# A decode attention block with a gated FFN: key and value tiles of four heads instead of two, three buffers instead of five, FFN and output weights last

## The chip, the cores and the metric

The kernel runs on one core of a Trainium2 chip (trn2). The metric is the device time of one execution in microseconds (us). A core has five engines with a queue each: TensorE (PE; its weight loads are listed as PEld), VectorE (DVE), ScalarE (ACT), GpSimd (POOL) and SyncE (SP), which here issues every DMA. Sixteen DMA engines, shared by all queues, move data between HBM and SBUF, the core's memory of 128 partitions; PSUM takes the results of TensorE.

## The reference

```python
q = (x @ wq)                       # x: [4, 1, 512], wq: [512, 32 heads * 128]
scores = einsum(q, k_cache) * 128 ** -0.5      # k_cache, v_cache: [4, 32, 4096, 128]
o = einsum(softmax(scores), v_cache)
a = o.reshape(4, 1, 4096) @ wo                 # wo: [4096, 512]
b = (gelu(x @ w_gate) * (x @ w_up)) @ w_down   # inner width 1792
g = sigmoid((x * gate_w).sum(-1, keepdims=True))
out = g * a + (1 - g) * b
```

All is float32. There are 4 batch entries with one query each; each has 32 heads with keys and values of their own, 4096 rows of 128 numbers. The two caches are 537 MB of the 565 MB that are read, and each number of them is used once.

## The kernel before, in words

**Tiles.** A key tile holds two heads of one batch entry (`HT = 2`): each head's 4096 rows lie over 64 partitions, 64 rows (`R`) of 128 numbers in each, so a partition gets 32 KB in one piece and a tile is 4 MB. Value tiles have the same layout. There are 64 tiles of each kind (index `i`: head pair `g = i // 4`, batch entry `b = i % 4`). All big loads share five places of 32 KB per partition (`NB = 5`, pool `kv`): the two halves of wq, keys, values, w_gate, w_up and w_down.

**Order.** The kernel is written in a manual schedule: on each engine the instructions stand in the order of the Python text, and an instruction waits for the data it reads and for the place that it writes. SP issues the big loads in the order of the list `loads`: wq in two halves (L62), then keys one tile ahead of values (L60), w_gate and w_up (L64) after the tiles 19 and 20, w_down (L69) last. Beside them go x (L95), gate_w in 13 small pieces (L104), and wo in 16 loads of 512 KB in rows of 2 KB, one for each head pair (L91).

**Scores.** The queries are computed at the start (L154 products with wq, L162 transposes, L164 copies into `QT`). `q_spread` (L177, L180) lays the queries of two heads for all four batch entries over the partitions, in `QB`. `products` (L192) multiplies 14 rows of a key tile by the query on DVE into a buffer `pr`, and `sums` (L198) adds each row up on DVE; 8 of the 64 rows (buffer `pa`) are added up by ACT instead (L201). In the last two tiles ACT adds up 24.

**Softmax.** `max_a` takes each partition's maximum (L217) and turns it into one row by a PE transpose (L219). `soft_max` takes the maximum of each head (L224), spreads it by PE (L227), copies it (L229) and has ACT compute the exponentials and their sums (L232) into one of three weight buffers `PM`. `soft_sum` (L239) adds up the sums over partitions.

**Values.** `pv` (L257) multiplies weights by values: 16 products of 128x512, four at a time on four column groups of PE, each recorded twice, so 32 records a tile. `o_out` copies the result (L264) and gathers the heads (L268); `weigh` (L277, L280) divides by the sums, and `project_a` (L250) multiplies by the rows of wo that belong to the two heads, adding up over the head pairs in `a_acc`.

**FFN.** `ffn_up` (L299), `ffn_gelu` (L307 to L320) run between the tiles 20 and 22, in a place of the pool. `ffn_down` (L250, `b_acc`) runs in parts around the last value tile. The last instructions are the gate's two products (L368, L372) and the store (L373).

**Loop.** In iteration `i` the program order is: first products of tile `i`, softmax of tile `i - 1`, products and sums of tile `i`, the next load, `pv(i - 1)`, the next load, `o_out(i - 1)`, `max_a(i)`, then the small loads and every fourth time `q_spread`.

Of the kernel before, what the change touches and what calls it, by code (L numbers as in the profile page):

```python
# [17 lines left out]
def tile_gated_mix(ctx: ExitStack, tc: tile.TileContext, x, kc, vc, wq, wo, w_gate, w_up, w_down, gate_w, out):  # L18
    nc = tc.nc
# [5 lines left out]
    C4 = DM // 4  # L25
    HT = 2
    PH = P // HT
    R = S // PH
    NT = B * H // HT
    NB = 5  # L30
    TW = R * D
    RJ = 4

    MANY = (((56, 64),), ((0, 14), (14, 28), (28, 42), (42, 56)), ("A0", "D0", "D1", "D2", "D3"))
    LAST = (((40, 48), (48, 56), (56, 64)), ((0, 14), (14, 28), (28, 40)), ("A0", "A1", "D0", "A2", "D1", "D2"))
    NL = 2
    FFN_AT = 20
    FG = 512
    GW_CUTS = (15, 14, 13, 12, 11, 10, 9, 8, 7, 6, 5, 4, 14)
# [3 lines left out]
    consts = ctx.enter_context(tc.tile_pool(name="consts", bufs=1))  # L43
    kv = ctx.enter_context(tc.tile_pool(name="kv", bufs=NB))
    work = ctx.enter_context(tc.tile_pool(name="work", bufs=2))
    ps2 = ctx.enter_context(tc.tile_pool(name="ps2", bufs=2, space=PSUM))
    ps1 = ctx.enter_context(tc.tile_pool(name="ps1", bufs=1, space=PSUM))
    ctx.enter_context(tc.manual_schedule())

# [3 lines left out]
    def load(kind, i):  # L53
        t = T[kind, i] = kv.tile([P, TW], F32, name="kv")
        if kind in "kv":
            h, b = HT * (i // B), i % B
            src = (kc if kind == "k" else vc)[b, h:h + HT].rearrange("h (p r) d -> (h p) (r d)", p=PH)
            n = 2 if (kind, i) == ("v", NT - 1) else 1
            for s in range(n):
                nc.sync.dma_start(t[:, s * TW // n:(s + 1) * TW // n], src[:, s * TW // n:(s + 1) * TW // n])  # L60
        elif kind == "q":
            nc.sync.dma_start(t, wq.rearrange("(p c) n -> p (c n)", c=KC)[:, i * TW:(i + 1) * TW])  # L62
        elif kind == "f":
            nc.sync.dma_start(t[:, :KC * F], (w_gate, w_up)[i].rearrange("(p c) n -> p (c n)", c=KC))  # L64
        else:
            for f0 in range(0, F, FG):
                f1 = min(f0 + FG, F)
                n = (f1 - f0) // P
                nc.sync.dma_start(t[:, f0 // P * DM:(f0 // P + n) * DM],  # L69
                                  w_down[f0:f1].rearrange("(p i) n -> p (i n)", i=n))  # L70

    loads = [("q", 0), ("q", 1), ("k", 0)]
    for i in range(NT):
        if i + 1 < NT:
            loads.append(("k", i + 1))
        loads.append(("v", i))
        if i in (FFN_AT - 1, FFN_AT):
            loads.append(("f", i - FFN_AT + 1))
    loads.append(("d", 0))
    loads = iter(loads)  # L80

    def load_next():
        n = next(loads, None)
        if n:
            load(*n)

    WO = {}

    def load_wo(g):
        WO[g] = work.tile([P, HT, DM], F32, name="wo_sb")  # L90
        nc.sync.dma_start(WO[g], wo[g * HT * D:(g + 1) * HT * D, :].rearrange("(h p) n -> p h n", p=P))  # L91

    load_next()
    x_sb = consts.tile([B, DM], F32)
    nc.sync.dma_start(x_sb, x.rearrange("b s d -> (b s) d"))  # L95
    load_next()
    for _ in range(NB - 2):
        load_next()
    gw = consts.tile([P, KC], F32)
    load_wo(0)  # L100

    def load_gw(j):
        s = slice(sum(GW_CUTS[:j]), sum(GW_CUTS[:j + 1]))
        nc.sync.dma_start(gw[s], gate_w.rearrange("(p c) -> p c", c=KC)[s])  # L104

    ident = consts.tile([P, P], F32)
    make_identity(nc, ident)
    ones = consts.tile([P, P], F32)  # L110
    nc.vector.memset(ones, 1.0)

    sel = consts.tile([P, RJ, HT], F32)
    nc.vector.tensor_reduce(sel.rearrange("p j h -> p (j h)"),
                            ident.rearrange("p (c m) -> p m c", c=4)[:, :RJ * HT, :], axis=AX.X, op=OP.add)

    PM = [consts.tile([P, R, HT], F32, name=f"pm{j}") for j in range(3)]
    RS = [consts.tile([P, B, HT], F32, name=f"rs{j}") for j in range(2)]
    for t in PM + RS:
        nc.vector.memset(t, 0.0)  # L120


    xT_ps = ps2.tile([P, KC, B], F32, name="sm")
    for c in range(KC):
        nc.tensor.transpose(xT_ps[:, c, :], x_sb[:, c::KC], ident[:B, :B])

    xT = consts.tile([P, KC, 4, B, 8], F32)
    for c in range(KC):
        nc.vector.tensor_copy(xT[:, c], xT_ps[:, c, None, :, None].to_broadcast([P, 4, B, 8]))
    xT = xT.rearrange("p c j b k -> p c (j b k)")  # L130
    g_cols = consts.tile([P, 2], F32)

    def gate():
        z = ps2.tile([P, 1], F32, name="sm")
        for c in range(KC):
            nc.tensor.matmul(z, xT[:, c, :], gw[:, c:c + 1], start=c == 0, stop=c == KC - 1)
        ez = work.tile([P, 1], F32, name="m1")
        nc.scalar.activation(ez, z, AF.Exp, scale=-1.0)
        gd = work.tile([P, 1], F32, name="nb")
        nc.vector.tensor_scalar(gd, ez, 1.0, None, op0=OP.add)  # L140
        nc.vector.reciprocal(g_cols[:, 0:1], gd)
        nc.vector.tensor_scalar(g_cols[:, 1:2], g_cols[:, 0:1], -1.0, 1.0, op0=OP.mult, op1=OP.add)


    PO = [ps1.tile([P, RJ, D], F32, name=f"po{j}") for j in range(2)]
    HG = H // 4
    HB = HG // 2
    q_sb = work.tile([P, HG, D], F32, name="wo_sb")
    for c in range(KC):
        w = T["q", c // 2].rearrange("p (c n) -> p c n", c=2)[:, c % 2, :]  # L150
        for s in range(2):
            for j in range(4):
                n0 = (j * HG + s * HB) * D
                nc.tensor.matmul(PO[s][32 * j:32 * j + 32].rearrange("p j d -> p (j d)"), xT[:, c, :32],  # L154
                                 w[:, n0:n0 + HB * D], start=c == 0, stop=c == KC - 1)
    for s in range(2):
        nc.scalar.activation(q_sb[:, s * HB:(s + 1) * HB, :], PO[s], AF.Copy)
    QT = consts.tile([P, 4, HG, B], F32)
    for s in range(2):
        ps = ps1.tile([P, HB, P], F32, name="q")  # L160
        for a in range(HB):
            nc.tensor.transpose(ps[:, a, :], q_sb[:, s * HB + a, :], ident)  # L162
        for a in range(HB):
            nc.vector.tensor_copy(QT[:, :, s * HB + a, :],  # L164
                                  ps[:, a, :].rearrange("p (j b k) -> p j b k", j=4, b=B)[:, :, :, 0])
    QT = QT.rearrange("p j a b -> p (j a) b")
    for _ in range(2):
        load_next()


    QB = {}

    def q_spread(g):
        ps = ps1.tile([P, B, D], F32, name="q")
        for b in range(B):
            for h in range(HT):
                nc.tensor.matmul(ps[h * PH:(h + 1) * PH, b, :], QT[:, HT * g + h, b:b + 1].to_broadcast([P, PH]),  # L177
                                 ident, start=True, stop=True)
        QB[g] = work.tile([P, B, D], F32, name="qb")
        nc.scalar.activation(QB[g], ps, AF.Copy)  # L180


    SC = {}
    dump = consts.tile([P, D], F32)

    def products(i, o):
        a, d, _ = LAST if i >= NT - NL else MANY
        r0, r1 = (a if o[0] == "A" else d)[int(o[1])]
        g, b = divmod(i, B)
        n = r1 - r0  # L190
        t = work.tile([P, n, D], F32, name="pa") if o[0] == "A" else work.tile([P, n, D], F32, name="pr", bufs=1)
        nc.vector.tensor_tensor(t, T["k", i].rearrange("p (r d) -> p r d", d=D)[:, r0:r1],  # L192
                                QB[g][:, b:b + 1, :].to_broadcast([P, n, D]), op=OP.mult)
        return t, r0, r1

    def sums(i, o, t, r0, r1):
        if o[0] == "D":
            nc.vector.tensor_reduce(SC[i][:, r0:r1], t, axis=AX.X, op=OP.add)  # L198
        else:
            for r in range(r0, r1):  # L200
                nc.scalar.activation(dump, t[:, r - r0, :], AF.Copy, accum_out=SC[i][:, r:r + 1])  # L201

    def scores_a(i):
        SC[i] = work.tile([P, R], F32, name="sc")
        return products(i, "A0")

    def scores(i, first):
        sums(i, "A0", *first)
        for o in (LAST if i >= NT - NL else MANY)[2][1:]:
            sums(i, o, *products(i, o))  # L210


    MT = {}

    def max_a(i):
        m1 = work.tile([P, 1], F32, name="m1")
        nc.vector.tensor_reduce(m1, SC[i], axis=AX.X, op=OP.max)  # L217
        MT[i] = ps2.tile([1, P], F32, name="sm")
# [177 lines left out]
```

## Time and profile before

| | |
|---|---|
| time, median of 3 runs | 1328.2 us (1328.17 to 1328.27) |
| span of the profiled execution, first to last instruction | 1328.7 us |
| instructions | 10291 |
| read from HBM | 564.67 MB, 425 GB/s over the span |
| DVE busy | 1142.8 us (86%) |
| PE busy | 544.3 us (41%), granted clock 0.648 of full speed in the mean |

The profile is of one execution of its own; its span is 0.5 us over the median of the runs, so a time worked out inside the profile is about 0.5 us more than what the runs would show. In a row of a timeline stand the start, the duration, the engine, the line, the operation, the tile written and the tile read, the shape and the count; in brackets how long the engine had been idle and what ended that. A row of the groups has the total busy time and the mean duration in ns behind the bar. A row of a DMA queue has the packets, the MB, and the time that the packets took as a share of sixteen engines' time. A packet is one contiguous run of bytes that one DMA engine moves.

### The profile page before, as it was taken

The page shows a single profiled execution, that of the slowest core. Times are in us where ns is not written, and L with a number is a line of the kernel's source. Part 1 is how long each engine was busy: PE and PEld are TensorE (multiplying, and loading weights), DVE is VectorE, ACT ScalarE, POOL GpSimd, SP SyncE. Part 2 cuts the span into 40 slices and gives each one's busy share as a digit, 9 for nine tenths or more (in the row PEclk, how much of TensorE's full clock was granted, in tenths as well). Part 3 has the DMA queues.
Part 4 walks back from the last instruction along what each step waited for, and adds up shares of the span by engine and source line. Part 5 has one row for each costly group of instructions (what it writes and reads, how often), then busy time and mean ns, then how long its engine had stood idle before and what let it go on. Part 6 is the DMA issues. An engine that isn't in the chain of part 4 may idle for free.

```text
span 1328.7 us, 10291 instructions
## 1 busy us (share of the span) xinstructions
PE 544.3 (41%) x3690; PEld 191.0 (14%) x3690; DVE 1142.8 (86%) x783; ACT 338.6 (25%) x1499; POOL 0.7 (0%) x6
## 2 busy tenths in 40 slices
PE   4243443443442553343344243343343344353345
PEld 1011111111110121111111111111111111111112
DVE  0999898898898679889889889889889889889874
ACT  0222222222222122312312212212312312212233
POOL 0000000000000000000000000000000000000000
PEclk9665766666666666766766665675665666665666
DMA  9999999999999999999999999999999999999996
GB/s 411 426 426 433 432 427 427 438 427 428 428 436 427 428 430 434 428 432 427 434 426 432 428 432 433 426 431 429 433 426 430 436 426 427 439 427 427 426 436 275
DMA packets 24414, 565.33 MB, mean 425 GB/s; under 512 B 2712, under 2 KB 2728, under 8 KB 6956
## 3 DMA queue, kind: packets, MB, share of 16 engines
q1 hardware_dynamic: 24364, 564.69, 99.2%
q8 instruction: 29, 0.48, 0.1%
q14 instruction: 21, 0.17, 0.0%
HBM read 564.67 MB, written 0.01 MB: 425 GB/s over the span
## 4 chain that ended last, share of the span: by engine, by line
DMA 71%; DVE 22%; PE 5%; issue 1%; another core or an unknown queue 0%; ACT 0%; SPq 0%; DVEq 0%; ACTq 0%
DMA kv<-in_A_k_cache 50%; DMA kv<-in_A_v_cache 21%; DVE pr L192 11%; DVE sc L198 9%; PE po L257 5%; DVE pa L192 2%; DVE m L224 0%; PE b_acc L250 0%; SPq L60 0%; PE oT L268 0%; ACT pm L232 0%; DVE ot L280 0%; ACT o L264 0%; SPq L62 0%
## 5 line engine op out<-in xcount | busy, mean ns | idle before, releaser
L257 PE MATMUL po<-kv,pm 128*8 128x512 f32 x2048 | 369.0, 887 | 489.3 <-DMA kv<-in_A_v_cache 482.2
L198 DVE TENSOR_REDUCE sc<-pr 128x14 f32<-128x1792 f32 x254 | 512.5, 2018 | 8.7
L192 DVE TENSOR_TENSOR pr<-kv,qb 128x1792 f32<-128x1792 f32 x254 | 512.3, 2017 | 6.4
L264 ACT ACTIVATE o<-po 128x512 f32<-128x512 f32 x64 | 38.2, 597 | 573.2 <-PE po L257 573.2
L192 DVE TENSOR_TENSOR pa<-kv,qb 128x1024 f32<-128x1024 f32 x68 | 83.2, 1224 | 108.6 <-DMA kv<-in_A_k_cache 108.5
L257 PEld LDWEIGHTS po<-kv,pm 128*8 128x8 f32 x2048 | 67.3, 117 | 738.6 <-issue 711.1
L201 ACT ACTIVATE dump<-pa 128x128 f32<-128x128 f32 x544 | 168.3, 309 | 18.1 <-DVE pa L192 1.5
L201 ACT ACTIVATION_READ_ACCUMULATOR dump<-pa 128x1 f32 x544 | 101.3, 186 | 0.0
L268 PE MATMUL oT<-sel,o 128*128 128x2 f32 x512 | 67.4, 254 | 45.5 <-ACT o L264 45.5
L227 PE MATMUL sm<-m,ones 1*64 1x1 f32 x256 | 23.3, 245 | 152.6 <-DVE m L224 152.6
L229 ACT ACTIVATE nb<-sm 128x1 f32<-128x1 f32 x64 | 10.9, 171 | 291.8 <-PE sm L227 291.7
L268 PEld LDWEIGHTS oT<-sel,o 128*128 128x128 f32 x512 | 61.9, 191 | 107.9 <-ACT o L264 107.9
L219 PE MATMUL sm<-ident,m 128*1 128x128 f32 x64 | 18.9, 295 | 72.4 <-DVE m L217 72.2
L232 ACT ACTIVATE pm<-sc,nb 64x64 f32<-64x64 f32 x128 | 44.9, 351 | 2.9
L227 PEld LDWEIGHTS sm<-m,ones 1*64 1x64 f32 x256 | 17.9, 192 | 169.2 <-DVE m L224 166.9
L232 ACT ACTIVATION_READ_ACCUMULATOR pm<-sc,nb 64x1 f32 x128 | 23.7, 185 | 0.0
L180 ACT ACTIVATE qb<-q 128x512 f32<-128x512 f32 x16 | 9.6, 597 | 50.3 <-PE q L177 50.3
L217 DVE TENSOR_REDUCE m<-sc 128x1 f32<-128x64 f32 x64 | 14.1, 220 | 6.6
L224 DVE TENSOR_REDUCE m<-sm 1x2 f32<-1x128 f32 x64 | 17.3, 270 | 2.6 <-PE sm L219 2.6
L177 PE MATMUL q<-ident,QT 128*64 128x128 f32 x256 | 18.7, 291 | 0.6 <-DVE QT L164 0.6
L250 PE MATMUL a_acc<-wo_sb,ot 128*32 128x128 f32 x256 | 16.9, 412 | 0.0
L219 PEld LDWEIGHTS sm<-ident,m 128*1 128x1 f32 x64 | 5.1, 80 | 75.6 <-issue 36.9
(49 smaller groups left out, 99.8 us busy)
## 6 DMA issues: line engine op xcount, KB each, us to landing
kv<-in_A_k_cache SPq DMA_DIRECT2D x64, 4096.0 KB, 42.5
kv<-in_A_v_cache SPq DMA_DIRECT2D x63, 4096.0 KB, 33.8
kv<-in_A_wq SPq DMA_DIRECT2D x2, 4096.0 KB
wo_sb<-in_A_wo SPq DMA_DIRECT2D x16, 512.0 KB, 43.1
kv<-in_A_v_cache SPq DMA_DIRECT2D x2, 2048.0 KB
kv<-in_B_w_gate SPq DMA_DIRECT2D x1, 3584.0 KB
kv<-in_B_w_up SPq DMA_DIRECT2D x1, 3584.0 KB
kv<-in_B_w_down SPq DMA_DIRECT2D x3, 1024.0 KB, 28.6
```

Of the source, the lines that this page charges most:

```text
L177: nc.tensor.matmul(ps[h * PH:(h + 1) * PH, b, :], QT[:, HT * g + h, b:b + 1].to_broadcast([P, PH]), ident, start=True, stop=True)
L192: nc.vector.tensor_tensor(t, T["k", i].rearrange("p (r d) -> p r d", d=D)[:, r0:r1], QB[g][:, b:b + 1, :].to_broadcast([P, n, D]), op=OP.mult)
L198: nc.vector.tensor_reduce(SC[i][:, r0:r1], t, axis=AX.X, op=OP.add)
L201: nc.scalar.activation(dump, t[:, r - r0, :], AF.Copy, accum_out=SC[i][:, r:r + 1])
L219: nc.tensor.transpose(MT[i], m1, ident)
L224: nc.vector.tensor_reduce(m2, MT[i].rearrange("o (h p) -> o h p", h=HT), axis=AX.X, op=OP.max)
L227: nc.tensor.matmul(nbp[h * PH:(h + 1) * PH, :], ones[:1, :PH], m2[:, h:h + 1], start=True, stop=True)
L232: nc.scalar.activation(PM[i % 3][s, :, h], SC[i][s, :], AF.Exp, bias=nb[s, :], scale=scale, accum_out=RS[g % 2][s, b, h:h + 1])
L250: nc.tensor.matmul(acc[32 * c:32 * c + 32, :], t, w[:, c * C4:(c + 1) * C4], start=start, stop=stop)
L257: nc.tensor.matmul(PO[i % 2][32 * c:32 * c + M].rearrange("p j d -> p (j d)"), p[:, j * M:(j + 1) * M], T["v", i][:, j * N:(j + 1) * N], s ...
L264: nc.scalar.activation(o, PO[i % 2], AF.Copy)
L268: nc.tensor.matmul(OT[g][:, b, :], o[:, j, :], sel[:, j, :], start=j == 0, stop=j == RJ - 1)
```

## The change

The body is rewritten around other tiles.

- **Tiles of four heads.** `HT = 4`: a head lies over 32 partitions, 128 rows in each, so that each partition gets 64 KB in one piece, a tile is 8 MB, and there are 32 of each kind. The pool has three places of 64 KB, which begin at an address fixed by a filler. wq is one tile. A tile's keys are loaded, then its values; the third load behind a tile goes into that tile's place, and waits until the tile has been read for the last time.
- **Products in place.** DVE multiplies a whole key tile by the query in one instruction, writing over the keys, and adds up all 128 rows in a second one. ACT adds up rows only in the last tile (32 of 128), where DVE works in four parts.
- **Softmax.** The maximum of a partition is laid out by a 32x32 transpose on DVE and the maximum of a head taken there, negated; the queries are scaled beforehand. The exponentials are four ACT instructions, one for each head, and there is one weight buffer. The PE transpose and spread and the ACT copy are gone.
- **Values.** 32 products a tile as before in shape. The result is copied and one product (`wide`) adds the column groups up into one PSUM tile for the four batch entries; after four tiles `quotients` takes the heads apart and divides. The projection by wo moves behind the loop.
- **Weights last.** Behind the last value tile come w_gate and w_up as one tile, w_down with the first 18 of 32 rows of wo a partition, and the other 14 rows in five pieces (4, 4, 3, 2, 1 rows). The whole FFN and the whole projection are computed behind the last quotient. gate_w is one load of four rows, and the gate is computed at the start, ahead of the queries.

```diff
-    HT = 2
+    HT = 4
-    NB = 5
+    PIECES = (4, 4, 3, 2, 1)
+    CH = 32
+    BASE = 24576
...
+    filler = front.tile([P, (BASE - 16512 - used) // 4], F32)
+    kv = ctx.enter_context(tc.tile_pool(name="kv", bufs=3))
...
+    def load_kv(kind, i):
+        nc.sync.dma_start(place((kind, i)), heads(kc if kind == "k" else vc, i))
...
+    for i in range(NT):
+        LOADS.append(lambda i=i: load_kv("k", i))
+        LOADS.append(lambda i=i: load_kv("v", i))
+    LOADS += [load_ffn_up, load_down, load_last]
...
+    def multiply(i, r0, r1):
+        k = keys(i)[:, r0:r1]
+        nc.vector.tensor_tensor(k, k, QB[:, i % B, None, :].to_broadcast([P, r1 - r0, D]), op=OP.mult)
+    def add_up(i, r0, r1):
+        nc.vector.tensor_reduce(SC[:, r0:r1], keys(i)[:, r0:r1], axis=AX.X, op=OP.add)
...
+    def weights(i):
...
+        nc.vector.tensor_reduce(m1, SC, axis=AX.X, op=OP.max)
...
+        nc.vector.transpose(mt, m1.to_broadcast([P, 32]))
...
+        nc.vector.tensor_reduce(nm, mt, axis=AX.X, op=OP.max, negate=True)
+        for h in range(HT):
+            s = slice(h * PH, (h + 1) * PH)
+            nc.scalar.activation(PM[s, :, h], SC[s, :], AF.Exp, bias=nm[s, :], scale=1.0,
+                                 accum_out=RS[s, b, h:h + 1])
...
+    for i in range(NT):
+        g, b = divmod(i, B)
+        last = i == NT - 1
+        multiply(i, 0, CH if last else R)
+        if i > 0:
+            if b == 0:
+                totals(g - 1)
+            values(i - 1)
+            load_next()
+        if b == 0 and i > 0:
+            quotients(g - 1)
+        if b == B - 1 and not last:
+            spread(g + 1)
+        if last:
+            add_up_beside(i, 0, CH)
+            for r in range(CH, R, CH):
+                multiply(i, r, r + CH)
+                add_up(i, r, r + CH)
+        else:
+            add_up(i, 0, R)
+        weights(i)
+        load_next()
+    load_next()
+    totals(NG - 1)
+    values(NT - 1)
+    load_next()
+    quotients(NG - 1)
...
+    for s, u in enumerate((u0, u1)):
+        up = PO[s][:, :FG]
+        for c in range(KC):
+            for j in range(4):
+                n0 = (s * KC + c) * F + j * FG
+                nc.tensor.matmul(up[32 * j:32 * j + 32], xT[:, c, :], f[:, n0:n0 + FG],
+                                 start=c == 0, stop=c == KC - 1)
+        nc.scalar.activation(u, up, AF.Copy)
...
+    early = [(hT[:, i, :], T["d"][:, i * DM:(i + 1) * DM]) for i in range(DR)]
+    early += [(OW[:, :, i], T["d"][:, (DR + i) * DM:(DR + i + 1) * DM]) for i in range(W1)]
+    for n, (l, r) in enumerate(early):
+        c = n % 4
+        nc.tensor.matmul(a[32 * c:32 * c + B], l, r, start=n < 4, stop=n >= len(early) - 4)
+    a_sb = back.tile([P, DM], F32, name="gs")
+    nc.scalar.activation(a_sb, a, AF.Copy)
...
+    for i in range(W1, WR):
+        for c in range(4):
+            r0 = (i - W1) * DM + c * P
+            nc.tensor.matmul(acc[32 * c:32 * c + 32], OX[:, i - W1].rearrange("p b k -> p (b k)"),
+                             T["w"][:, r0:r0 + P], start=False, stop=i == WR - 1)
```

Names used below: k0 to k31 and v0 to v31 are the new tiles; `values`, `totals`, `quotients`, `spread` are the functions above; `up` are the products with w_gate and w_up; the early products are the 32 with w_down and the first part of wo; the last products are the 56 with the rest of wo.

More of the change, by code (lines that the diff above doesn't have):

```diff
@@ L48, in tile_gated_mix @@
+    used = 5 * 512 + 512 + 448 + 2048 + 64 + 2048
+    filler = front.tile([P, (BASE - 16512 - used) // 4], F32)
+    kv = ctx.enter_context(tc.tile_pool(name="kv", bufs=3))
+    back = ctx.enter_context(tc.tile_pool(name="back", bufs=1))
+    ps = ctx.enter_context(tc.tile_pool(name="ps", bufs=1, space=PSUM))
     ctx.enter_context(tc.manual_schedule())
     T = {}
[L53 to L70, printed above, removed]
@@ L72, in tile_gated_mix, with place @@
-    loads = [("q", 0), ("q", 1), ("k", 0)]
-    for i in range(NT):
[L74 to L80, printed above, removed]
-    def load_next():
[L83 to L91, printed above, removed]
+    def place(key):
+        T[key] = kv.tile([P, TW], F32, name="kv")
+        return T[key]
@@ L114, in tile_gated_mix @@
[L114 to L123, printed above, removed]
+    nc.vector.memset(wide, 0.0)
+    nc.vector.memset(PM, 0.0)
+    nc.vector.memset(RS, 0.0)
@@ L124, in tile_gated_mix @@
+    xT_ps = ps.tile([P, KC, B], F32, name="sm", bufs=2)
     for c in range(KC):
         nc.tensor.transpose(xT_ps[:, c, :], x_sb[:, c::KC], ident[:B, :B])
-    xT = consts.tile([P, KC, 4, B, 8], F32)
     for c in range(KC):
[L129 to L142, printed above, removed]
@@ new lines, in tile_gated_mix @@
+    nc.tensor.matmul(z_ps, ones[:B, :], zd, start=True, stop=True)
+    gates = back.tile([P, 2, B], F32)
+    ez = back.tile([P, B], F32)
+    nc.scalar.activation(ez, z_ps, AF.Exp, scale=-1.0)
+    nc.vector.tensor_scalar(ez, ez, 1.0, None, op0=OP.add)
+    nc.vector.reciprocal(gates[:, 0], ez)
+    nc.vector.tensor_scalar(gates[:, 1], gates[:, 0], -1.0, 1.0, op0=OP.mult, op1=OP.add)
+    PO = [ps.tile([P, RJ * D], F32, name=f"po{s}") for s in range(2)]
+    QP = ps.tile([P, B * D], F32, name="q")
@@ L166, in tile_gated_mix @@
[L166 to L174, printed above, removed]
-        for b in range(B):
[L176 to L180, printed above, removed]
@@ L196, in sums @@
[L196 to L210, printed above, removed]
@@ L373, in tile_gated_mix @@
+    res = back.tile([P, P], F32, name="res")
+    nc.vector.tensor_copy(res, acc)
     nc.sync.dma_start(out.rearrange("b s (c n) -> c (b s) n", c=4), res[::8])
```

323 lines of the change are left out of this document (146 added, 177 removed).

## The prediction

> **What bounds the kernel now.** I read the engines' shares, the DMA lines and the chain of waits on the page first.
>
> ```profile
> PE 544.3 (41%) x3690; PEld 191.0 (14%) x3690; DVE 1142.8 (86%) x783; ACT 338.6 (25%) x1499; POOL 0.7 (0%) x6
> DMA  9999999999999999999999999999999999999996
> DMA packets 24414, 565.33 MB, mean 425 GB/s; under 512 B 2712, under 2 KB 2728, under 8 KB 6956
> q1 hardware_dynamic: 24364, 564.69, 99.2%
> q8 instruction: 29, 0.48, 0.1%
> DMA 71%; DVE 22%; PE 5%; issue 1%; another core or an unknown queue 0%; ACT 0%; SPq 0%; DVEq 0%; ACTq 0%
> ```
>
> The DMA engines are full in every slice but the last, and DVE, next, has 14% to spare. So DMA bounds it, and as the change reads the same bytes, only three things can move the end: the cost of a packet beside its bytes, how evenly the sixteen engines finish, and what follows the last byte. Next, the windows at the end and the starts of two key tiles in the timeline.
>
> ```profile
> 1313.00:1320.00 7.00, 5.81 (x32) 1.16 (x36) 0.00 (x0) 1.04 (x5) 0.00 (x0) 0.52 0.62 256
> 1320.00:1322.00 2.00, 2.00 (x44) 1.26 (x36) 0.00 (x0) 0.60 (x1) 0.00 (x0) 0.96 0.09 37
> 32.45 1.23 DVE L192 TENSOR_TENSOR pa<-kv,qb 128x1024 f32<-128x1024 f32 x1 [2.08 <-DMA kv<-in_A_k_cache]
> 1294.35 1.23 DVE L192 TENSOR_TENSOR pa<-kv,qb 128x1024 f32<-128x1024 f32 x1 [4.57 <-DMA kv<-in_A_k_cache]
> ```
>
> The last three columns of a window are granted PE clock, DMA share and GB/s. The share falls to 0.62 and to 0.09: engines with equal shares of the bytes end up to 9 us apart, the slowest at about 1322.2. Behind it the kernel takes 6.5 us to its end at 1328.7.
>
> **Packets.** The DMA view of two windows gives packets, MB and share of sixteen engines: the second half of wq (32 KB rows), then w_down (8 and 4 KB rows).
>
> ```profile
> q1 hardware_dynamic: 95, 3.11, 102.9%
> DMA packets 360, 3.31 MB, mean 414 GB/s; under 512 B 40, under 2 KB 40, under 8 KB 56
> q1 hardware_dynamic: 359, 3.29, 98.6%
> ```
>
> The first (14 to 21 us) is 1.029 x 7 x 16 / 95 = 1.213 us a packet, 37.0 ns a KB. The second (1305 to 1313) is 126.2 us for 319 data packets of 10.3 KB in the mean, 38.4 ns a KB. The difference over 1/10.3 - 1/32.8 is 20 ns a packet beside its bytes; packet ends stretched by neighbours are in it. So the constant is 0 to 20 ns; I take 9, nearest the middle. A 64 KB packet then takes 2 x 1.213 - 0.009 = 2.417 us, and an 8 MB tile, eight packets on each engine, 19.34 us. An engine moves 520 such packets in place of 1032 for keys, values and wq: 4.6 us less (0 to 10). Whole rows of wo and half as many loads: 1 us less (0 to 2).
>
> **From k0 to the last key tile.** Before, 1294.4 - 32.4 = 1262 us lie between these arrivals. In them an engine moves 125 tiles of 4 MB (8 x 1.213 each: 1213), w_gate and w_up (7.3 MB at that rate: 17) and wo (8.4 MB: 20), together 1250. The slowest lost 12 us on top. One cause shows in the DMA view of 54.5 to 59.5 us:
>
> ```profile
> q8 instruction: 1, 0.02, 1.4%
> ```
>
> That packet held one engine for 1.4% of 5 x 16 us, 1.1 us. Packets of instructions (0.48 MB for 7380 PE records, 65 B each) hit one engine at a time; the load's end waits for the engine hit most. The change has 1293 matmul calls for 1845 (the 1024 value products stay), so some 20 such packets, 16 ahead of the last key tile, for 28; ACT and DVE issue far less. 12 x 16 / 28 is 7 us.
>
> **The reserve.** Evening-out needs loads queued ahead. Before, three or four tiles are. With three places v(i+1) is issued only when k(i) has been added up.
>
> ```profile
> L198 DVE TENSOR_REDUCE sc<-pr 128x14 f32<-128x1792 f32 x254 | 512.5, 2018 | 8.7
> L192 DVE TENSOR_TENSOR pr<-kv,qb 128x1792 f32<-128x1792 f32 x254 | 512.3, 2017 | 6.4
> L192 DVE TENSOR_TENSOR pa<-kv,qb 128x1024 f32<-128x1024 f32 x68 | 83.2, 1224 | 108.6 <-DMA kv<-in_A_k_cache 108.5
> 45.92 2.02 DVE L192 TENSOR_TENSOR pr<-kv,qb 128x1792 f32<-128x1792 f32 x1
> 47.97 0.33 SPq L60 DMA_DIRECT2D kv<-in_A_k_cache  x1
> 0.74 0.40 SPq L62 DMA_DIRECT2D kv<-in_A_wq  x1
> DMA  0000000000000000099999098700700000009997
> ```
>
> Two sizes give 1.033 ns an element and 166 ns; 16384 elements take 17.1 us, product and sum 34.3. SP issues 0.03 us behind the last reader (47.94 to 47.97). The first load, issued at 0.74, shows its first data in the slice at 1.7 (0 to 4 us in 40 slices) and is under way on all engines by 2.5: 1 to 2 us. So v(i+1) can start about 36.2 us after k(i) has arrived and is due after 38.7: 1.5 to 3 us of reserve, less 0.5 where `quotients` puts a reciprocal and a product between. That just covers one instruction packet, so faster engines are held within it of the slowest; I add 1 us to the 7, bounds 5 to 14. k(i+1) is no trouble: its place is free once `values(i-1)` ends, some 8 us early. Behind SP's waiting load stand only later loads, all due later.
>
> **What costs nothing inside the loop.** The new DVE steps for a tile, product, sum and 0.7 us of maxima, are 35.0 of the 38.7 us that its two loads take, so the softmax steps that go (PE transpose, spread, ACT copy) and ACT's 8 sums a tile that move to DVE change no end: the two loads cover them with 3.7 us, and beyond that every us costs 31, as in the first rival. The one weight buffer makes the exponentials of tile i wait for `values(i-1)`, done 10 us into the tile when they are due at 35; behind them on ACT stands nothing, and `values(i)`, which waits for them, has until v(i)'s place is due, 58 us behind k(i): 9 us to spare. `QB` is written again by ACT behind the product of every fourth tile, 17 us ahead of its next reader. The projection and the copies by group of four leave PE and ACT, which had 59% and 75% idle.
>
> k0 arrives one more 4 MB later, 41.9. The query chain begins when x lands behind 8 MB of wq, 22.7 (one 4 MB ahead of 32.4), and the gate's matmul ahead of the wq products adds 2 us; by the rows of before (products 10, copies, transposes, spreads 5) `QB` is ready at about 41: covered by 1 us, and if not, the first tile starts late by as much, once. Then 62 tiles to k31: 62 x 19.34 + 8 = 1207, at **1249**. v31 (19.3), w_gate and w_up (17.0), the next tile (19.4) and the last pieces (8.7) end the DMA at 1313.4, against 1322.2. Their places are in time: that of k31 is read by 31 us behind it and due at 36, that of v31 by 44 and due at 56.
>
> **Behind k31.** What was hidden in the middle now stands in line.
>
> ```profile
> 1314.37 6.46 PE L257 MATMUL po<-kv,pm 128*8 128x512 f32 x32 [1.19 <-ACT pm L232]
> 53.26 5.55 PE L257 MATMUL po<-kv,pm 128*8 128x512 f32 x32 [1.19 <-ACT pm L232]
> 57.35 0.10 PEld L257 LDWEIGHTS po<-kv,pm 128*8 128x8 f32 x4 [0.56 <-issue]
> 57.78 0.10 PEld L257 LDWEIGHTS po<-kv,pm 128*8 128x8 f32 x4 [0.33 <-issue]
> 1315.18 0.16 PEld L257 LDWEIGHTS po<-kv,pm 128*8 128x8 f32 x4 [0.70 <-issue]
> 1316.04 0.16 PEld L257 LDWEIGHTS po<-kv,pm 128*8 128x8 f32 x4 [0.70 <-issue]
> 472.05 6.09 PE L299 MATMUL q<-kv,xT 128*32 128x512 f32 x32 [1.09 <-DVE q L295]
> L264 ACT ACTIVATE o<-po 128x512 f32<-128x512 f32 x64 | 38.2, 597 | 573.2 <-PE po L257 573.2
> L232 ACT ACTIVATE pm<-sc,nb 64x64 f32<-64x64 f32 x128 | 44.9, 351 | 2.9
> L217 DVE TENSOR_REDUCE m<-sc 128x1 f32<-128x64 f32 x64 | 14.1, 220 | 6.6
> 1321.63 1.05 PE L268 MATMUL oT<-sel,o 128*128 128x2 f32 x8
> 1324.18 1.49 PE L250 MATMUL b_acc<-kv,hT 128*32 128x128 f32 x48
> L307 DVE TENSOR_TENSOR kv<-u 128x512 f32<-128x512 f32 x1 | 0.7, 694 | 2.0 <-PE q L299 2.0
> 1326.12 0.66 SPq L373 DMA_DIRECT2D out<-res  x1
> ```
>
> Four records side by side take 0.43 us at full clock (57.35 to 57.78) and 0.86 at half. `values(31)` is 16 such groups: 5 us at half clock, as both tile rows begin, the rest at full, 9.7. In us from k31, hops of 0.1 between engines included: seven DVE steps of 32 rows (4.4 each) to 31.0, ACT's 32 sums hidden behind them; maximum, transpose, maximum 0.9 (the transpose, not in the trace, 0.1 to 1; I take 0.2, as the L217 row); four exponentials 2.0; `values` to 43.7; copy, `wide` product, copy, four picks (as L268), quotient, `L` and four matmuls 5.9, to 49.6; `up`, 16 groups of 7/8 size, 6 to 9, I take 7.5; copy, tanh, two products, transpose, `hT` 3.6, to 60.7; 32 early products, 7 to 10, take 7.9; copy and adding up 1.2; the 56 last products at 0.031 a record 3.5; copy and store 3.0, to **76.3**. Bounds 72 to 84. The DMA is done at 64.4, so nothing here waits for it any more, and this chain sets the end, 12 us behind the last byte where it was 6.5.
>
> The sum by its terms: -5.6 (packets), -4 (skew: 12 to 8), +6 (tail): 1328.7 - 3.6, or 1249 + 76.3 = 1325.2. The runs lie 0.5 under their profile: **1324.7 us**.
>
> **A rule against it.** wq is read before in rows that lie 64 KB apart, and the first DMA row above is that load, at the full 1.213 us a packet. The Trainium skill, "DMA: Bandwidth & Descriptors", section "Latency and other measured facts", warns of row pitches at large powers of two (207 GB/s at 512 KiB). The row speaks against it at 64 KB. The Trainium skill, "Runtime: NRT & Kernel Launch", section "Instruction fetch mechanics", calls the cost of a new block of instructions mostly hidden; by this rule the skew would not follow the count of instructions. The 1.1 us row says that it is not hidden from the loads.
>
> **The rivals.** *Reserve too small* (slower): if the instructions of DVE at nine times the size, or the way from issue to first byte, cost 2 to 3 us more, DMA idles at each v; the point is 38.7 us from k(i)'s arrival to v(i+1)'s start, and each us beyond costs 31 us (1356); just short of it, each instruction packet costs up to 1.5 us (1332 to 1345). For it: no row has one instruction of 16384 elements. Against: size and time go straight in two rows. 0.15. *Cold clock* (slower): the gaps behind k31 keep PE at half clock: `values` 13.7, `up` 12, early 13.7, last 7, together 18 more, 1342. For it: clock 0.52 up to 1320 while PE worked; against: 0.96 right after. 0.10. *DMA sets the end* (faster): the chain is 8 us shorter than counted; 1313.4 + 4 - 0.5 = 1317. 0.08. *Rows don't do what they say* (same): a 64 KB row goes as two packets of 1.213, which brings 4.6 us back: 1329. 0.04. *Fetches don't matter* (same; the second rule): the 12 us stay whatever the count of instructions: 1324.7 + 4 = 1329. 0.03. *Row pitch* (slower; the first rule): should 64 KB rows slow keys and values, each per cent of rate is 12 us; 5% gives 1385. 0.02. The forecast has 0.58, its own range 1318 to 1331.
>
> **How the numbers follow.** Some 0.2% (2.7 us) can be told from no change, so faster means under 1325.5 and slower over 1330.9. The forecast's range lies some six tenths below the first, nearly all the rest within: 0.36 faster, 0.20 same, 0.02 slower. With the rivals faster has 0.44, same 0.27, slower 0.29. The likeliest time stays 1324.7. The range 1316 to 1342 leaves out the worse half of the first rival, half of the second and the last, under 0.2; its ends also hold the bounds of the packets (0 to 10), the skew (5 to 14) and the tail (72 to 84) taken two at a time.
>
> **What would show it.** Right: 8320 packets of 64 KB at about 2.417 us, k31's product at about 1249, DMA windows full to 1305, `values(31)` 44 us behind k31, FFN products behind that, the end 12 us behind the last load. Wrong: SP's loads of v issued late with empty DMA slices at each tile (the first rival), PE clock 0.5 in the last 30 us (the second), product or sum longer than 17.3 us.

## The result and the profile after

The changed kernel takes 1337.1 us (median of four runs, 1336.9 to 1339.4) against 1328.2 for the kernel before: 1.0069 times as long, 95% interval 1.0054 to 1.0083. The forecast was 1324.7, a little faster than before; the kernel became slower. The page of the changed kernel, the lines that answer to those shown of before:

```profile
span 1335.0 us, 6193 instructions
PE 387.6 (29%) x2590; PEld 100.4 (8%) x2590; DVE 1133.3 (85%) x221; ACT 119.8 (9%) x408; POOL 0.7 (0%) x6
DMA  9999999999999999999999999999999999999995
DMA packets 10719, 565.07 MB, mean 423 GB/s; under 512 B 1196, under 2 KB 1212, under 8 KB 1604
q1 hardware_dynamic: 10692, 564.69, 98.6%
q8 instruction: 20, 0.33, 0.1%
q14 instruction: 7, 0.06, 0.0%
DVE 44%; DMA 38%; PE 14%; ACT 3%; issue 1%; DVEq 0%; SPq 0%; ACTq 0%
```

PE, ACT and the count of packets fell as the edits say, and the DMA row still shows nines to the last slice. The chain of waits does not look like that of before: DVE holds 44% of it where it held 22%. A DMA that is busy in every slice can still wait for DVE, if each wait is much shorter than a slice (33 us). The share alone does not show it: with four places in the kernel before, where nothing is lost (below), DVE holds 36%. The timeline of DVE and SP over one tile and the start of the next shows where the DMA can wait, with the start of the last key tile below:

```profile
591.98 17.22 DVE L188 TENSOR_TENSOR kv<-kv,QB 128x16384 f32<-128x16384 f32 x1 [3.41 <-DMA kv<-in_A_k_cache]
600.63 0.33 SPq L75 DMA_DIRECT2D kv<-in_A_k_cache  x1
609.31 17.22 DVE L191 TENSOR_REDUCE SC<-kv 128x128 f32<-128x16384 f32 x1
626.56 0.33 SPq L75 DMA_DIRECT2D kv<-in_A_v_cache  x1
630.91 17.23 DVE L188 TENSOR_TENSOR kv<-kv,QB 128x16384 f32<-128x16384 f32 x1 [3.59 <-DMA kv<-in_A_k_cache]
...
1256.26 4.42 DVE L188 TENSOR_TENSOR kv<-kv,QB 128x4096 f32<-128x4096 f32 x1 [3.99 <-DMA kv<-in_A_k_cache]
```

Product and sum take 17.2 us each, as forecast, and SP issues the load of v 34.6 us behind the arrival of the keys, 4.35 us ahead of the end of the next keys (630.91). The loads of k are issued 30 us ahead. From k0's product (42.34) to k31's (1256.26) it is 1213.9 us; 496 packets of 2.414 us, the usual distance of two packets on one DMA engine, are 1197.3. So 16.6 us are lost there where the forecast had 8.

The issues in the DMA view, before and after, say the same in one number, the time from issue to landing:

```profile
kv<-in_A_v_cache SPq DMA_DIRECT2D x63, 4096.0 KB, 33.8
```

```profile
kv<-in_A_k_cache SPq DMA_DIRECT2D x32, 31.2
kv<-in_A_v_cache SPq DMA_DIRECT2D x32, 24.2
```

Eight packets of 1.213 us are 9.7, so before a value load lay some 24 us in the queue ahead of its own bytes; now, with 19.3 us of bytes, 4.9.

The end of the changed kernel, in the timeline:

```profile
1290.77 9.60 PE L225 MATMUL po<-kv,PM 128*16 128x512 f32 x64
1306.05 7.92 PE L294 MATMUL po<-kv,xT 128*32 128x448 f32 x64
1317.81 5.85 PE L313 MATMUL q<-kv,hT 128*4 128x512 f32 x26 [3.85 <-DVE hT L306]
...
1323.50 4.03 PE L313 MATMUL q<-kv,ow 128*4 128x512 f32 x34
1328.56 3.24 PE L323 MATMUL g<-kv,o 128*32 128x128 f32 x112
1332.19 0.66 SPq L327 DMA_DIRECT2D out<-res  x1
```

The last packet of a load ends at 1320.2; the end is 14.8 us behind it and 78.7 behind k31.

### The profile page after: what moved, and what is told of

It reads as the page before. It is cut to its first block, busy times and chain, and to the rows that moved or that the text cites. A ratio compares the mean times of both kernels' runs of the same rounds, so it can differ in the third digit from the quotient of the medians.

```text
span 1335.0 us, 6193 instructions
## 1 busy us (share of the span) xinstructions
PE 387.6 (29%) x2590; PEld 100.4 (8%) x2590; DVE 1133.3 (85%) x221; ACT 119.8 (9%) x408; POOL 0.7 (0%) x6
## 4 chain that ended last, share of the span: by engine, by line
DVE 44%; DMA 38%; PE 14%; ACT 3%; issue 1%; DVEq 0%; SPq 0%; ACTq 0%
DMA kv<-in_A_k_cache 38%; DVE SC L191 22%; DVE kv L188 21%; PE po L225 12%; ACT PM L207 3%; PE q L313 1%; PE po L294 1%; DVE m L200 0%; DVE mt L202 0%; DVE nm L204 0%; PE g L323 0%; DVE OT L242 0%; DVE ri L235 0%; ACT o L228 0%; PE g L231 0%
## 5 line engine op out<-in xcount | busy, mean ns | idle before, releaser
L188 DVE TENSOR_TENSOR kv<-kv,QB 128x16384 f32<-128x16384 f32 (+1 forms) x35 | 551.6, 15761 | 122.0 <-DMA kv<-in_A_k_cache 122.0
L191 DVE TENSOR_REDUCE SC<-kv 128x128 f32<-128x16384 f32 (+1 forms) x34 | 547.0, 16088 | 2.6
L225 PE MATMUL po<-kv,PM 128*16 128x512 f32 x2048 | 298.6, 749 | 668.2 <-ACT PM L207 668.2
L207 ACT ACTIVATE PM<-SC,nm 32x128 f32<-32x128 f32 x128 | 65.9, 515 | 775.6 <-DVE nm L204 772.9
L225 PEld LDWEIGHTS po<-kv,PM 128*16 128x16 f32 x2048 | 62.5, 114 | 890.1 <-ACT PM L207 683.2
L228 ACT ACTIVATE o<-po 128x512 f32<-128x512 f32 x32 | 19.1, 597 | 309.0 <-PE po L225 309.0
L231 PE MATMUL g<-o,wide 128*64 128x512 f32 x64 | 34.3, 618 | 25.1 <-ACT o L228 25.1
L207 ACT ACTIVATION_READ_ACCUMULATOR PM<-SC,nm 32x1 f32 x128 | 24.9, 195 | 0.0
L200 DVE TENSOR_REDUCE m<-SC 128x1 f32<-128x128 f32 x32 | 9.2, 286 | 1.2
L195 ACT ACTIVATE QX<-kv 128x128 f32<-128x128 f32 x32 | 9.9, 309 | 1.0
```

Source lines behind the costliest of these rows:

```text
L188: nc.vector.tensor_tensor(k, k, QB[:, i % B, None, :].to_broadcast([P, r1 - r0, D]), op=OP.mult)
L191: nc.vector.tensor_reduce(SC[:, r0:r1], keys(i)[:, r0:r1], axis=AX.X, op=OP.add)
L195: nc.scalar.activation(dump, keys(i)[:, r, :], AF.Copy, accum_out=SC[:, r:r + 1])
L200: nc.vector.tensor_reduce(m1, SC, axis=AX.X, op=OP.max)
L207: nc.scalar.activation(PM[s, :, h], SC[s, :], AF.Exp, bias=nm[s, :], scale=1.0, accum_out=RS[s, b, h:h + 1])
L225: nc.tensor.matmul(po[32 * c:32 * c + M], p[:, j * M:(j + 1) * M], T["v", i][:, j * RJ * D:(j + 1) * RJ * D], start=j < 4, stop=j >= n - 4)
```

## The experiments

Theory A: v(i+1) is issued too late, at the tiles the DMA engines that are done first wait for it, and their delays add up. Rival B: the long rows or the big tiles lose the time themselves. Theory C: behind k31 the compute sets the end. "k0 to k31" and "behind k31" are from the profiled runs; ratios are to the kernel before.

| kernel | us | ratio (95%) | k0 to k31 | q14 packets | behind k31 |
|---|---|---|---|---|---|
| again (the changed kernel) | 1338.0 | 1.0067 (1.0044 to 1.0090) | 1214.5 | 7 | 75.4 |
| beside | 1329.3 | 1.0001 (0.9991 to 1.0010) | 1207.0 | 19 | 77.7 |
| late | 1352.6 | 1.0182 (1.0159 to 1.0204) | 1233.6 | 8 | 78.7 |
| ffn | 1328.3 | 0.9996 (0.9985 to 1.0006) | 1212.7 | 7 | 68.9 |
| fetch | 1338.9 | 1.0071 (1.0054 to 1.0088) | 1219.4 | 7 | 78.8 |
| beside_fetch | 1328.6 | 0.9992 (0.9983 to 1.0002) | 1206.2 | 19 | 78.1 |
| both | 1319.5 | 0.9928 (0.9914 to 0.9943) | 1207.0 | 19 | 68.2 |
| half | 1334.0 | 1.0038 (1.0025 to 1.0050) | (below) | 9 | (below) |
| both40 | 1326.4 | 0.9981 (0.9971 to 0.9991) | 1214.2 | 27 | 69.0 |
| both_act | 1326.3 | 0.9979 (0.9969 to 0.9989) | 1213.6 | 27 | 68.9 |
| poolm | 1362.9 | 1.0263 (1.0243 to 1.0282) | 1251.7 | 8 | 68.5 |
| pools | 1314.1 | 0.9885 (0.9869 to 0.9902) | 1202.0 | 9 | 68.5 |
| four (before, 4 places) | 1330.0 | 1.0006 (0.9996 to 1.0017) | | | |
| three (before, 3 places) | 1351.0 | 1.0165 (1.0128 to 1.0202) | | | |

**The reserve.** The changed kernel again:

> The changed kernel as it is, beside the three that follow, so that they share one measure. Every theory expects 1337 +- 1.5 us, k31's product starting near 1256 and 1214 us between the starts of the products of k0 and k31.

It came out as expected, with runs from 1333.7 to 1340.4. Then v earlier, and v later:

```diff
-            add_up(i, 0, R)
+            add_up_beside(i, 0, 24)
+            add_up(i, 24, R)
```

> ACT adds up 24 of the 128 rows of every key tile beside DVE, so that DVE is done with a tile 3.2 us earlier and the load of the next values is issued 3.2 us earlier. Theory A (no reserve: the load of v(i+1) is issued so late that a delay of any one DMA engine is added to the whole): the 1214 us between k0 and k31 fall to about 1206, as before the slowest engine alone counts; time 1329 to 1331. Rival B (the 64 KB rows or the 8 MB loads lose the time whenever they are issued): 1337, or 1 to 3 more for some six further packets of ACT instructions.

```diff
             add_up(i, 0, R)
+            add_up(i, 0, 8)
```

> DVE adds up the first 8 rows of every tile but the last a second time, 1.2 us more ahead of the load of the next values; the DMA is asked for the same bytes. Theory A: next to no reserve is left, so of 31 x 1.2 = 37 us at least half appears: 1357 to 1374, all of it ahead of k31. Rival B: DVE stays within the 38.7 us that two loads take, so 1337 to 1339.

With v issued 3.2 us earlier 8.8 us are gone, 7.5 of them between k0 and k31 by the profiles. With v issued 1.2 us later the time grows by 14.6: less than the 20 to 37 expected, so a little reserve had been left. DVE still stood idle for 2.7 to 3.7 us ahead of the keys (the three tiles from 599 us on), and the DMA was asked for the same. A holds, B falls. The timeline of the first of the two:

```profile
586.87 17.23 DVE L188 TENSOR_TENSOR kv<-kv,QB 128x16384 f32<-128x16384 f32 x1 [7.12 <-DMA kv<-in_A_k_cache]
604.20 14.02 DVE L191 TENSOR_REDUCE SC<-kv 128x104 f32<-128x13312 f32 x1
618.28 0.33 SPq L75 DMA_DIRECT2D kv<-in_A_v_cache  x1
625.42 17.23 DVE L188 TENSOR_TENSOR kv<-kv,QB 128x16384 f32<-128x16384 f32 x1 [6.34 <-DMA kv<-in_A_k_cache]
```

The issue lies 7.1 us ahead of the next keys now, and that tile took 38.55 us, its sixteen packets of 2.414 (38.62) and no more.

**Fewer places in the kernel before.** `NB = 4` and `NB = 3` in the kernel before, nothing else.

> The kernel before with four places of 4 MB instead of five. A load of keys then waits for the keys two tiles back and is due 11 us behind their sum, a load of values for those two tiles back. By the theory of the reserve this is far more than the 2.4 to 4 us from issue to data: no change, 1328 to 1330. If the number of places or the bytes on hand matter by themselves (16 MB here, 24 MB in the changed kernel): as much loss as there or more, 1337 and over.

> The kernel before with three places of 4 MB. As in the changed kernel the values of a tile wait for its own keys: these are added up some 17 to 18 us behind their arrival, and the two loads of a tile take 19.4 us, so 1.5 to 2.5 us remain for a way from issue to data that takes 2.4 to 4. By the theory of the reserve 0.5 to 2 us are lost at each of 64 tiles: 1360 to 1450. If the long rows or the big tiles cost the time: little change, 1328 to 1335.

Four places change nothing. Three cost 22.8 us with the old tiles and the old rows (two runs, 1347.8 and 1354.1), less than expected (0.36 us a tile), but on that side: it is the wait for the tile's own keys that costs, not the size of the tile. Both expectations put the way from issue to data at 2.4 to 4 us; where it can be read off ("poolm", below), the packets start 0.96 to 1.9 us behind the issue and the first ones end 3.9 to 4.5 us behind it.

**Packets of instructions on PE.** The prediction held these to be the cause of the loss.

```diff
             values(i - 1)
             load_next()
+            for _ in range(32):
+                nc.tensor.matmul(extra[:8], ident[:, :8], ones[:, :8], start=True, stop=True)
```

> Behind the values of every tile stand 32 more products of 128x8 by 8 columns on PE, into a place of PSUM that nothing reads: some 4000 more PE records, 16 more instruction packets, and no other work in anyone's way (PE has 20 us idle in each tile). Theory A (held at every v load, delays of different engines add up; the 27 packets of instructions and 16 us lost so far make about half of 1.1 us count for each): 16 x 0.5 = 8 us more, 1343 to 1348. Rival B (each engine loses its own time only): 16 packets over 16 engines, 1 to 2 us more, 1338 to 1340.

> The same 32 products a tile, and ACT adds up 24 rows of each tile, so that the load of v is issued 3.2 us earlier. Theory A: the reserve covers one packet of instructions, so the further ones cost the slowest engine alone: 1 to 4 us over the 1329.3 of the kernel with ACT's 24 rows and without these products, 1330 to 1333, where they cost 8 without the reserve. Rival B: the same addition with and without reserve.

The page has the packets, 36 in place of 20:

```profile
q8 instruction: 36, 0.59, 0.2%
q14 instruction: 7, 0.06, 0.0%
```

They cost 0.8 us by the medians without the reserve and nothing with it. (The profiled run of the first was the longest of its four, 1342.0; its 1219.4 stands against medians that hardly differ.) The runs of the two kernels without the reserve spread over 5 and 7 us, so some 4 us could hide there; with the reserve the intervals leave at most 1.5 us for the 16 packets. So PE's packets are not the main part of what is lost: this part of theory A and of the prediction falls.

**Rows of 32 KB.** Each load of keys and values in two.

> Each load of keys and values is two loads of 32 KB rows (first and second half of each row), one behind the other: 8192 packets more. If a packet costs what the steady distances show (two of 1.213 against one of 2.414 us): 512 x 0.012 = 6 us more, 1342 to 1345; the 4.6 us of the prediction would be 1341. If the count of packets does not matter: 1337.

Neither: 3 to 4 us less than the changed kernel. The start of the last two key tiles in its timeline:

```profile
1219.65 17.23 DVE L190 TENSOR_TENSOR kv<-kv,QB 128x16384 f32<-128x16384 f32 x1 [3.71 <-DMA kv<-in_A_k_cache]
...
1254.98 8.76 DVE L190 TENSOR_TENSOR kv<-kv,QB 128x4096 f32<-128x4096 f32 x2
```

k31 starts 35.3 us behind k30 where a tile takes 39: DVE's first quarter of it needs the first half only, and so everything behind k31 came 3 to 4 us earlier (the end is 77.8 us behind that start). Between k0 and k30 it took 1177.1 us against 1174.6 (1216.93 less 42.34) in the changed kernel and 1175.6 in its second profile, "again", so the packets cost some 1.5 to 2.5 us in thirty tiles. Two packets of 32 KB come 1.209 us apart here, 0.004 more for a pair than one of 64 KB.

**The end.** w_gate and w_up ahead of v31, their products behind `values(30)`, the gelu behind the maxima of tile 31:

```diff
+    LOADS.insert(-1, load_ffn_up)
-    LOADS += [load_ffn_up, load_down, load_last]
+    LOADS += [load_down, load_last]
...
                 add_up(i, r, r + CH)
+            ffn_up()
...
+    hT = ffn_gelu()
     load_next()
     totals(NG - 1)
     values(NT - 1)
```

> w_gate and w_up are loaded ahead of v31 and not behind it, their products stand on PE behind the values of tile 30, the copies behind ACT's sums, and the gelu on DVE behind the maxima of tile 31, beside the values of tile 31. Theory C (the end is set by the chain of compute behind k31): products 7.9 and gelu 3.6 us leave it, v31 comes 1.8 us later than the weights need it, so the chain would end 9.7 us earlier and the last byte (landing 14.5 us ahead of the end) with some 6 us of work behind it takes over: 8 us less, 1328 to 1330. Rival D (the DMA, or the clock of PE, sets it): the early products start on a cold PE and take 4 us more, or the end keeps its distance to the last byte: 1333 to 1337.

Theory C holds: 9.7 us less, behind k31 68.9 us in place of 75.4 and 78.7. The end is 4.6 us behind the last load now (1323.8 for 1319.2). With both edits:

> ACT adds up 24 rows of each tile, and w_gate and w_up come ahead of v31 with their products and the gelu beside the scores and values of tile 31. If the two losses are separate, one ahead of k31 and one behind it: 8.8 + 9.7 us less than 1337 to 1338, so 1318 to 1321, faster than the kernel before. If the loads only wait elsewhere (the last tiles come earlier, but the chain behind them or the last byte does not): 1323 to 1328.

1319.5: the two losses are separate, and each edit gives what it gave alone.

**More reserve, and a surprise.** ACT adds up 40 rows and starts earlier (`multiply(i, 0, 40)` and `multiply(i, 40, R)` in place of one product, `spread` behind ACT's sums):

> As the kernel with both edits (1319.5), but ACT adds up 40 rows of every tile instead of 24 and starts behind the product of those 40 rows (the product is in two parts; the spread of the next queries moves behind ACT's sums): DVE is done with a tile 2.1 us earlier still, so v is issued some 9.3 us ahead of the next keys' end instead of 7.2. If the way from issue to data together with the unevenness of the engines is what is lost at v, 24 rows leave 4 to 6 us of it (DMA engines idle 2.2 us and long packets 3.6 us each): 1315 to 1318. If 24 rows cover all that a reserve can cover, or ACT's further 1000 instructions cost as much as they bring: 1319 to 1321.

It got worse by 6.9 us, though v was issued 9.9 us ahead. The starts of the key tiles in the kernel with both edits, and below them the DMA view's rows of instruction packets for 627 to 664 us and for 705 to 742 us; between 588 and 625 and between 667 and 702 there is no such packet:

```profile
587.24 17.23 DVE L189 TENSOR_TENSOR kv<-kv,QB 128x16384 f32<-128x16384 f32 x1 [7.12 <-DMA kv<-in_A_k_cache]
625.79 17.23 DVE L189 TENSOR_TENSOR kv<-kv,QB 128x16384 f32<-128x16384 f32 x1 [6.34 <-DMA kv<-in_A_k_cache]
665.12 17.22 DVE L189 TENSOR_TENSOR kv<-kv,QB 128x16384 f32<-128x16384 f32 x1 [7.13 <-DMA kv<-in_A_k_cache]
703.70 17.23 DVE L189 TENSOR_TENSOR kv<-kv,QB 128x16384 f32<-128x16384 f32 x1 [6.12 <-DMA kv<-in_A_k_cache]
743.01 17.23 DVE L189 TENSOR_TENSOR kv<-kv,QB 128x16384 f32<-128x16384 f32 x1 [7.12 <-DMA kv<-in_A_k_cache]
```

```profile
q8 instruction: 1, 0.02, 0.2%
q14 instruction: 1, 0.01, 0.1%
...
q14 instruction: 2, 0.02, 0.1%
```

The tiles take 38.55, 39.33, 38.58 and 39.31 us: those with a packet on q14 are 0.7 us longer. Over the whole run the 15 tiles with such a packet take 39.3 us in the mean, the 15 without 38.6. q14 grows with ACT's instructions (7, 19, 27 packets with 0, 24 and 40 rows). It does not carry ACT's alone: the kernel before has 21 packets with 1499 ACT instructions, "beside" 19 with 1896. This makes theory F: ACT's packets cost what PE's do not.

```diff
+            for _ in range(32):
+                nc.scalar.activation(nil, ones[:, :1], AF.Copy)
```

> The kernel with both edits and ACT's 24 rows (1319.5), and 32 copies of one column on ACT in every tile but the first, behind the copy of `values`, where ACT is idle until the product ends: the load of v is issued at the same point, 7.2 us ahead of the next keys' end. About 1000 more ACT instructions are 8 more packets of ACT's instruction queue (q14), as many as the kernel with 40 rows has over the one with 24. Theory F (a q14 packet costs the whole some 0.65 us, as the tiles that hold one in the trace are 0.70 us longer and the others are not, while PE's packets on q8 cost nothing): 5 us more, 1323 to 1326. Rival G (the 40 rows lost their time by something else, an issue at a worse point or the split product): 1319 to 1320.5.

6.7 us more, 0.8 for each of eight packets, a little over F's bound; G falls. Then the reserve without ACT:

```diff
+            k = keys(i)[:, R - 24:]
+            nc.gpsimd.tensor_tensor(k, k, QB[:, i % B, None, :].to_broadcast([P, 24, D]), op=OP.mult)
+            multiply(i, 0, R - 24)
...
             add_up(i, 0, R)
```

> w_gate and w_up ahead of v31 as before, but ACT adds up no rows in the tiles 0 to 30: POOL multiplies the last 24 rows of every tile in one instruction beside DVE's product of the other 104, which is 3.2 us shorter. The same reserve as with ACT's 24 rows, and no further instructions. Theory F: the 12 packets of q14 that ACT's rows brought, 0.65 to 0.7 us each, are gone: 8 us less than 1319.5, 1311 to 1314, and next to nothing is lost between k0 and k31 (1198 to 1201 us). Rival G: 1319 to 1320. If POOL and DVE hinder each other at the memory, DVE's product is longer by what POOL takes, the reserve is gone, and the time is that with the weights' order alone, 1327 to 1330 or more.

```profile
588.15 17.22 DVE L192 TENSOR_REDUCE SC<-kv 128x128 f32<-128x16384 f32 x1 [6.54 <-POOL kv L283]
605.39 0.33 SPq L75 DMA_DIRECT2D kv<-in_A_v_cache  x1
606.64 14.03 DVE L189 TENSOR_TENSOR kv<-kv,QB 128x13312 f32<-128x13312 f32 x1 [0.48 <-DMA kv<-in_A_k_cache]
606.67 20.49 POOL L283 TENSOR_TENSOR kv<-kv,QB 128x3072 f32<-128x3072 f32 x1 [18.56 <-DMA kv<-in_A_k_cache]
```

A miss, and not by a hindrance: DVE's product takes 14.03 us beside POOL, as its size says (13312 x 1.033 + 166 ns = 13.9), but POOL takes 20.5 us and DVE waits 6.5 us for it, so the reserve was negative. With DVE's sum in two parts, `add_up(i, 0, R - 24)` and then `add_up(i, R - 24, R)`, nobody waits:

> As the kernel with POOL's 24 rows, but DVE adds up its own 104 rows first and POOL's 24 in a second instruction, so that POOL's 20.5 us end 7 us ahead of their reader. DVE is done with a tile 3.0 us earlier than in the changed kernel, as with ACT's 24 rows, with two more instructions in a tile instead of 48. Theory F (ACT's packets of instructions cost 0.65 to 0.85 us each): the tiles lose next to nothing, 1199 to 1203 us between k0 and k31, 1311 to 1315. Rival G (what is left after ACT's 24 rows is lost otherwise): 1319 to 1321.

```profile
585.23 14.03 DVE L189 TENSOR_TENSOR kv<-kv,QB 128x13312 f32<-128x13312 f32 x1 [6.65 <-DMA kv<-in_A_k_cache]
599.36 17.28 DVE L192 TENSOR_REDUCE SC<-kv 128x104 f32<-128x13312 f32 x2
616.66 0.33 SPq L75 DMA_DIRECT2D kv<-in_A_v_cache  x1
623.77 14.02 DVE L189 TENSOR_TENSOR kv<-kv,QB 128x13312 f32<-128x13312 f32 x1 [6.35 <-DMA kv<-in_A_k_cache]
```

1314.1 us, 1.15% (0.98 to 1.31) less than the kernel before and 1.7% less than the changed one; k0 to k31 is 1202.0 us, 4.7 over its packets. F holds. At 0.63 us for a packet (below) the q14 packets between 100 and 1200 us, 7, 16 and 23 in "pools", "both" and "both_act", would be 4.4, 10.1 and 14.5; lost were 4.7, 9.7 and 16.3. In "pools" that agreement is chance: its six tiles with such a packet take 38.7 us in the mean, the others 38.8. So the price holds for the packets that ACT's further instructions bring, and not for every packet of q14; what makes the 4.7 us was not followed up.

## Why the prediction was wrong

The forecast was 12.4 us short: 7.3 at k31 (1256.3 for 1249), 2.4 behind it, 2.4 by the step from profile to runs, the rest rounding and the run profiled.

- **Packets: right in size, mixed in cause.** 2.414 us for the 2.417 taken. But two 32 KB packets of the changed kernel cost 0.004 more than one of 64 KB, not 0.009, 2 us for all 512 pairs; what else made the distances of before 1.213 was not tried.
- **The cause of the 12 us before k31: wrong.** The step put 12 us down to 28 packets of instructions and scaled it by PE's calls, "ACT and DVE issue far less". PE's packets cost next to nothing, as the rival "Fetches don't matter" (0.03) had it for all of them; those that ACT's rows brought cost 0.63 to 0.85 us each, and the page of before has a row for that queue:

```profile
q14 instruction: 21, 0.17, 0.0%
```

  21 x 0.63 is 13 us, which would be the whole loss of before. But no run took the ACT sums out of that kernel, some of the 21 packets are not ACT's, and which engines they hit can't be followed in its trace, so what cost the 12 us of before stays open. "pools", with 20 and 9 packets of instructions for the changed kernel's 20 and 7, loses 4.7 us in all, so the 7 of this step were some 2 too many.
- **The reserve: the step that failed.** "That just covers one instruction packet, so faster engines are held within it of the slowest; I add 1 us to the 7". The issue came when it said (34.6 us behind the keys). The way to the first data had been right too. In "poolm" all engines but one had run dry when v was issued at 605.39; the windows there, with the DMA share and GB/s last (a packet counts where it starts):

```profile
604.00:605.00 1.00, 0.00 (x0) 0.00 (x0) 1.00 (x1) 0.00 (x0) 0.00 (x0) 0.50 0.01 0
605.00:606.00 1.00, 0.00 (x0) 0.00 (x0) 0.90 (x4) 0.00 (x0) 0.00 (x0) 0.50 0.00 0
606.00:607.00 1.00, 0.00 (x0) 0.00 (x0) 0.52 (x2) 0.72 (x3) 0.33 (x1) 0.50 2.86 983
```

  The packets start 0.96 to 1.9 us behind the issue, but each first one then takes 2.5 to 3.4 us in place of 2.41. What was missing: the reserve was counted to the end of the last engine, while engines that finish the keys 2 us or more ahead of it have next to none. Followed packet by packet between 50 and 1235 us, a DMA engine of the changed kernel is idle some 4 us in the mean and has packets that are some 11 us too long in all, nearly nine tenths of it in packets that start within 5 us behind an issue of v; in "pools" both are about 1 us. With 1202.0 us in "pools" for 1213.9, the late issue cost 12 us where 1 was added: the loss ahead of k31 was to fall from 12 to 8 us and was 16.6. This is the outcome of the first rival, "Reserve too small", whose weaker form had 1332 to 1345 (0.15 was too small a chance for it), but not by the ways that it named: DVE's instructions took 17.2 us and the first data 1 to 2 us, as forecast, and further packets of PE's instructions cost little.
- **The tail: right in its steps.** `values` began 34.5 us behind k31 and `up` at 49.8 (49.6). The early products took 9.7 us for 7.9, starting at half clock (0.50 granted from 1317.8 to 1322), and make 1.8 of the 2.4 us; they were inside their bounds. The DMA ended where it should, and the end was set by compute.
- **Profile and runs: wrong.** A run of before with the span of its profile, 1328.7 us, takes 1330.5; the runs near the median have spans of 1326.2 to 1326.7. In all 19 runs of before beside the first experiments the time is 1.7 to 1.9 us over the span, and in the changed kernel too (1336.9 for 1335.0). The step took 0.5 off where 1.9 had to be added.
- **The rules.** 64 KB rows at a pitch of 64 KB ran at full rate (2.414 us), so the pitch of the first rule does not matter here. The Trainium skill, "Runtime: NRT & Kernel Launch", section "Instruction fetch mechanics", calls the cost of crossing a block mostly hidden. For the loads beside it this held here of PE's packets (16 more for 0.8 us or nothing), not of those that ACT's instructions brought (8 more for 6.7 us).

## What to carry to other kernels

When a load waits for the tile that it replaces, count its reserve to the DMA engine that finishes first, not to the last one, and ask for several us more than the way from issue to data; the packed DMA row will not show that it is missing. The issue's time to landing, less the time of its own bytes, does: 4.9 us in the changed kernel, 7.1 in "pools" (26.4 less 19.3). DVE's share of the chain is no safe sign: 44% in the changed kernel, but 39% in "pools" too. An idle engine is not free cover if its help comes in many small instructions: ACT's 24 rows won 9 us, and POOL's in two instructions a tile won 5 more. An execution's span and its time should be compared run by run before a difference between profile and median is used.

## What the runs showed of the hardware that was not expected

A packet of q14, the queue that grows with ACT's instructions (8 KB, 0.31 us), delays the next packet of one DMA engine by 0.31 us and lengthens it by about as much. An engine can be followed where each packet starts at the end of the last one. In "both" eleven of the fourteen q14 packets from 80 to 898 us hit one and the same engine, and in "both_act" all five from 403 to 616 us hit one; PE's (16 KB, 0.9 us, 1.4 us of delay) went around, the first eight in "pools" over eight engines, and the seven of q14 there do not keep to one engine either. Delays on one engine add up, and those that go around are evened out: this fits these runs, but which engine takes which queue was not changed by any. POOL's product of two inputs takes 20.47 us for 128x3072, 6.7 ns an element and six times DVE's 1.03, without slowing DVE beside it.
